# Strided attention with a squared-ReLU feed-forward: long rows for v and k, larger vector operations, both PSUM banks of the attention in one operation, five blocks by seven products

## Chip, cores, metric

One core of one Trainium2 chip. The time is device microseconds from start to end of one execution; "span" is the profiled time from the first to the last instruction. Runs are compared with runs of the kernel before of the same rounds on the same chip. Where two runs of different rounds are compared with each other, their chips can differ, so the ratios to the kernel before are the safer measure.

## The reference

```python
q, k, v = (8, 8, 576, 64) each; w_in = (512, 2048); w_out = (2048, 512)
scores = q @ k.T / sqrt(64)
# heads 0-3: the last 32 positions ("loc"); heads 4-7: every 32nd position ("str")
attn = softmax(where(mask, scores, -1e9))
x = (attn @ v), heads side by side       # (8*576 = 4608 tokens, 512)
r = maximum(x @ w_in, 0)
out = (s * r * r + b) @ w_out            # (4608, 512), float32
```

## The kernel before

The kernel is unrolled. A planner in Python (`Plan`) has assumed costs of every operation and writes out a fixed order of instructions for each engine. A software layer then adds the semaphores. Attention goes batch by batch (`b`), two heads at a time (a "pair", `m`; `loc = m < 2`). The feed-forward goes in nine blocks of 512 tokens (`T`): first product L877 (`w_in`), relu and square, second product (`w_out`). Blocks from `SEVEN` on take their second product as seven half-size products of sums and differences instead of eight; a "block by seven products" below.

The eight PSUM banks are one tile each:

```python
    TB, SB, AB, F1B, F2B = 1, 2, 1, 2, 2
    ps = {tag: [psum.tile([128, PS], FP32, name=f"ps_{tag}{i}") for i in range(n)]
          for tag, n in (("t", TB), ("s", SB), ("a", AB), ("f1", F1B), ("f2", F2B))}
    # t: transposes; s: scores; a: attention times v ("AV"); f1, f2: the two products.
    # ... from batch 4 on AV uses a and t in turn
```

Scores, exponential and mask of one group (a third of a pair), and the division after AV:

```python
                def ex(eng):                      # one group into a p buffer of its own (6 buffers)
                    nc.scalar.activation(out=pt[0:nk, 0:2 * n]..., in_=st["s", g]..., func=AF.Exp, scale=scale)
                def ms(eng):
                    nc.vector.tensor_tensor(out=pt[0:nk, 0:2 * n], in0=pt[0:nk, 0:2 * n], in1=mask, op=ALU.mult)
# ... [cut]
                def rc(eng):
                    nc.vector.reciprocal(out=st["rec", e, j]..., in_=st["pa", e, j][0:nq, 0:per, D:D + 1])
                def mu(eng):
                    nc.vector.tensor_tensor(out=st["x"][:, j0:j0 + per, 64 * e:64 * e + 64],
                        in0=st["pa", e, j][0:nq, 0:per, 0:D], in1=st["rec", e, j]..., op=ALU.mult)
```

Loads and transposed keys. GpSimd issues the loads; before those of a batch it waits, by a copy of one element, for the transposed keys of the batch before:

```python
    def fetch_qk(b):
        for mm in range(2):
            if (b - 1, "kTs", mm) in loaded:
                nc.gpsimd.tensor_copy(out=gate[0:1, 2 + mm:3 + mm], in_=loaded[b - 1, "kTs", mm][0:1, 0, 0:1])
        load_qk(b)      # from batch 4 on, k comes in 4 loads of 72 KB, in the order the transpose wants
# ... [cut]
                nc.sync.dma_start_transpose(out=st["k"][:, LPAD:LPAD + S]..., in_=loaded[b, "kl"][...])
```

The softmax here doesn't subtract the row's maximum and nothing guards it: scores larger than these inputs give would overflow.

## Time and profile before

| | before |
|---|---|
| time, median | 311.7 us (311.1 to 312.3) |
| span of the profiled run | 309.0 us |
| TensorE standstill: before 30 us, 30 to 85, after 85 | 6.3, 3.1, 0.1 us |
| useful and clock-warming matmuls (288.2 + 5.1) | 293.3 us |

Standstill is worked out from the trace: the distance from each matmul's start to the next, less what its columns take at 2.4 GHz. The prediction below explains it and shows the lines. The groups of the division (busy us, mean ns, then idle time before them):

```profile
L611 DVE TENSOR_TENSOR x_nat<-ps_a,rec 72x256 f16<-72x256 f32 (+1 forms) x52 | 23.7, 456 | 0.6
L600 DVE RECIPROCAL rec<-ps_a 72x4 f32<-72x4 f32 (+1 forms) x52 | 9.1, 176 | 6.1 <-PE ps_a L585 5.5
```

VectorE waits for AV (5.5 us).

### The profile page before, as it was taken

The page shows a single profiled execution, that of the slowest core. Times are in us where ns is not written, and L with a number is a line of the kernel's source. Part 1 is how long each engine was busy: PE and PEld are TensorE (multiplying, and loading weights), DVE is VectorE, ACT ScalarE, POOL GpSimd, SP SyncE. Part 2 cuts the span into 40 slices and gives each one's busy share as a digit, 9 for nine tenths or more (in the row PEclk, how much of TensorE's full clock was granted, in tenths as well). Part 3 has the DMA queues.
Part 4 walks back from the last instruction along what each step waited for, and adds up shares of the span by engine and source line. Part 5 has one row for each costly group of instructions (what it writes and reads, how often), then busy time and mean ns, then how long its engine had stood idle before and what let it go on. Part 6 is the DMA issues. An engine that isn't in the chain of part 4 may idle for free.

```text
span 309.0 us, 6715 instructions
## 1 busy us (share of the span) xinstructions
PE 300.5 (97%) x2526; PEld 194.4 (63%) x2526; DVE 218.2 (71%) x575; ACT 178.3 (58%) x336; POOL 99.8 (32%) x146
## 2 busy tenths in 40 slices
PE   8899999989999999999999999999999999999994
PEld 3765655555656655556687755565677666766883
DVE  7567958799976877859755874589866366737653
ACT  1876945769736964668055736694945445356300
POOL 8562559934951592059202950000000000000000
PEclk9999999999999999999999999999999999999999
DMA  7999999998999699679998999842010100200313
GB/s 127 204 212 205 216 175 159 219 135 122 99 165 176 86 147 155 110 110 183 150 174 153 128 146 159 172 92 88 2 36 34 68 2 34 104 1 0 105 67 106
DMA packets 99940, 37.28 MB, mean 121 GB/s; under 512 B 81170, under 2 KB 95890, under 8 KB 99906
## 3 DMA queue, kind: packets, MB, share of 16 engines
q0 software_dynamic: 57200, 18.08, 60.9%
q1 hardware_dynamic: 42706, 18.76, 29.9%
q8 instruction: 20, 0.33, 0.5%
q14 instruction: 14, 0.11, 0.1%
HBM read 36.84 MB, written 10.32 MB: 153 GB/s over the span
## 4 chain that ended last, share of the span: by engine, by line
PE 82%; DMA 9%; DVE 4%; issue 2%; ACT 1%; POOL 1%; SPq 0%; DVEq 0%; POOLq 0%; ACTq 0%
PE ps_f L877 35%; PE ps_f L926 20%; PE ps_f L845 12%; DMA ql<-in_q_dram 6%; PE ps_s L531 4%; PE ps_a L585 2%; DMA w_out_sb<-in_v_dram 2%; PE ps_s L845 2%; PE ps_t L585 1%; PE ps_t L845 1%; PE ps_s L926 1%; PE ps_t L411 1%; DMA out_dram<-o 1%; PE ps_t L633 1%; DVE gT L908 1%
## 5 line engine op out<-in xcount | busy, mean ns | idle before, releaser
L877 PE MATMUL ps_f<-xT,w_in_sb 128*128 128x512 f16 (+1 forms) x632 | 148.0, 357 | 0.0
L899 ACT ACTIVATE u<-ps_f 128x512 f16<-128x512 f32 x137 | 81.1, 596 | 72.8 <-PE ps_f L877 69.5
L877 PEld LDWEIGHTS <-w_in_sb 128*128 128x128 f16 x640 | 68.1, 113 | 34.5
L926 PE MATMUL ps_f<-w_out_sb,gT 128*128 128x512 f16 x304 | 80.7, 379 | 0.2 <-DVE gT L908 0.2
L908 DVE TENSOR_TENSOR gT<-u 128x512 f16<-128x512 f16 x111 | 48.1, 438 | 31.7 <-ACT u L899 30.6
L926 PEld LDWEIGHTS <-gT 128*128 128x128 f16 x320 | 28.9, 98 | 23.2 <-DVE gT L908 0.5
L845 PEld LDWEIGHTS <-gT 128*128 128x128 f16 x320 | 31.0, 98 | 8.7
L845 PE MATMUL ps_f<-w_out_sb,gT 128*128 128x256 f16 x184 | 25.9, 273 | 0.0
L611 DVE TENSOR_TENSOR x_nat<-ps_a,rec 72x256 f16<-72x256 f32 (+1 forms) x52 | 23.7, 456 | 0.6
L547 ACT ACTIVATE p_loc<-ps_s 128x384 f16<-128x384 f32 x46 | 21.1, 493 | 5.1 <-PE ps_s L531 4.8
L547 ACT ACTIVATE p_str<-ps_s 72x432 f16<-72x432 f32 (+1 forms) x46 | 21.0, 485 | 3.2 <-PE ps_s L531 2.9
L585 PEld LDWEIGHTS <-p_str 72*128 72x128 f16 x256 | 15.5, 98 | 11.2 <-issue 1.4
L906 ACT ACTIVATE gT<-u 128x512 f16<-128x512 f16 x33 | 20.8, 630 | 1.0
L293 POOL DMA_DIRECT2D v_loc<-in_v_dram x28 | 20.6, 764 | 1.8 <-DVE qD_loc L315 1.8
L937 DVE SCALAR_TENSOR_TENSOR o<-ps_f,s_sb,bcs 128x512 f32<-128x512 f32 x19 | 14.1, 747 | 9.4 <-PE ps_f L926 9.2
L298 POOL DMA_DIRECT2D v_str<-in_v_dram x16 | 13.0, 815 | 10.7 <-PE ps_a L585 3.7
L555 DVE TENSOR_TENSOR p_str<-p_str,mask_str 72x432 f16<-72x432 f16 (+1 forms) x42 | 14.7, 360 | 1.3 <-ACT p_str L547 1.0
L555 DVE TENSOR_TENSOR p_loc<-p_loc,mask_loc 128x384 f16<-128x384 f16 x42 | 14.6, 360 | 1.2 <-ACT p_loc L547 0.9
L845 PEld LDWEIGHTS <-S 128*128 128x128 f16 x128 | 12.5, 98 | 3.2
L315 ACT COPY xT<-ps_t 128x576 f16<-128x576 f16 x9 | 5.7, 637 | 13.4 <-PE ps_t L633 13.4
L600 DVE RECIPROCAL rec<-ps_a 72x4 f32<-72x4 f32 (+1 forms) x52 | 9.1, 176 | 6.1 <-PE ps_a L585 5.5
L585 PEld LDWEIGHTS <-p_loc 128*128 128x128 f16 x192 | 10.1, 98 | 5.2 <-issue 0.7
(158 smaller groups left out, 406.4 us busy)
## 6 DMA issues: line engine op xcount, KB each, us to landing
out_dram<-o SPq DMA_DIRECT2D x34, 256.0 KB, 3.1
w_out_sb<-in_moe_w_out_dram POOLq DMA_DIRECT2D x4, 512.0 KB, 11.1
v_loc<-in_v_dram POOLq DMA_DIRECT2D x28, 72.0 KB, 7.8
ql<-in_q_dram POOLq DMA_DIRECT2D x6, 288.0 KB, 6.4
qs<-in_q_dram POOLq DMA_DIRECT2D x6, 288.0 KB, 6.2
ks<-in_k_dram POOLq DMA_DIRECT2D x6, 288.0 KB, 7.6
kl<-in_k_dram POOLq DMA_DIRECT2D x4, 288.0 KB, 8.9
kl<-in_k_dram POOLq DMA_DIRECT2D x16, 72.0 KB, 3.9
```

The lines of the kernel that those rows point to most:

```text
L293: nc.gpsimd.dma_start(out=vl[LPAD:128, h, :, 0:D], in_=v_band(b, h))
L547: nc.scalar.activation(out=pt[0:nk, 0:2 * n].rearrange("k t c -> k (t c)"), in_=st["s", g][0:nk, 0:2 * n * nq], func=AF.Exp, scale=scale)
L555: nc.vector.tensor_tensor(out=pt[0:nk, 0:2 * n], in0=pt[0:nk, 0:2 * n], in1=mask, op=ALU.mult)
L585: nc.tensor.matmul(out=st["a"][:, j % per, :], lhsT=st["pw", g][0:nk, i * nq:i * nq + WIDE], rhs=vt[0:nk, 2 * mm + e, j, :])
L611: nc.vector.tensor_tensor(out=st["x"][:, j0:j0 + per, 64 * e:64 * e + 64], in0=st["pa", e, j][0:nq, 0:per, 0:D], in1=st["rec", e, j][0:nq, ...
L845: nc.tensor.matmul(out=gts[name, T, t][:, 0] if halves else gts[name, T][:, t], lhsT=lhs(k, t), rhs=rhs(k), start=fresh and k == 0 and (ha ...
L877: nc.tensor.matmul(out=gts["h", T, ft][:, lo:hi], lhsT=w_in_sb[min(ft // 4, 2)][:, ct].rearrange("p (c x l) -> p c l x", x=128, l=4)[:, ma ...
L899: nc.scalar.activation(out=gts["u", T, ft], in_=gts["h", T, ft], func=AF.Relu)
L906: nc.scalar.activation(out=gts[T][:, ft, :], in_=u, func=AF.Square)
L908: nc.vector.tensor_tensor(out=gts[T][:, ft, :], in0=u, in1=u, op=ALU.mult)
L926: nc.tensor.matmul(out=gts[id_], lhsT=gts[T][:, ft, ts * 128:(ts + 1) * 128], rhs=w_out_sb[:, ft, cols], start=(ft == 0), stop=(ft == NFT ...
L937: nc.vector.scalar_tensor_tensor(out=o[:, 0:n], in0=gts[id_], scalar=s_sb[:, 0:1], in1=bcs[:, cols], op0=ALU.mult, op1=ALU.add)
```

## The change

The intent is to take fixed costs off VectorE and GpSimd and one eighth off another block's second product. Cut to its core:

```diff
-    NX = 4                       # x of four batches in a ring
+    NX = 3
-    p_bufs: 6 tiles of one group
+    p_bufs: 2 tiles of a whole pair
-    v_str = [... for i in range(NV)]      # two
+    v_str = const.tile([SQ, 4, ST, D + 1], FP16)     # one; v of the strided heads is loaded in long rows and cast
-          for tag, n in (("t", TB), ("s", SB), ("a", AB), ("f1", F1B), ("f2", F2B))}
+          for tag, n in (("s", SB), ("f1", F1B), ("f2", F2B))}
+    ps_at = psum.tile([128, 2, PS], FP32, name="ps_at")
+    ps["a"], ps["t"] = [ps_at[:, 0]], [ps_at[:, 1]]
+    AV_WIDE = KB_DMA             # from batch 4 on
+        def both_banks(e, group):
+            got = ps_at[0:nq, :, 0:per * (D + 1)].rearrange("q u (j d) -> q u j d", d=D + 1)
+            ... one reciprocal and one multiplication for both banks
-    SEVEN = 5
+    SEVEN = 4
+            def ms(eng):         # one mask over the whole pair, behind its three exponentials
+                nc.vector.tensor_tensor(out=pt[0:nk], in0=pt[0:nk], in1=mask, op=ALU.mult)
+            def sq(eng):         # one square over two blocks of 512
+                g = gts[T][:, pair[0]:pair[0] + 2, :]
+                nc.vector.tensor_tensor(out=g, in0=u, in1=u, op=ALU.mult)     # or on ScalarE
# keys of the local heads from batch 4 on: one load of 288 KB, a copy that pairs the heads,
# the DMA transpose into kTl, and a spread into the order that the scores want
-                nc.sync.dma_start_transpose(out=st["k"][:, LPAD:LPAD + S]..., in_=loaded[b, "kl"]...)
+                nc.sync.dma_start_transpose(out=loaded[b, "kTl"][:, mm], in_=paired[b, "k"][:, mm]...)
+        def k_spread(eng):
+            copy_on(eng, out=st["k"][:, LPAD:LPAD + S]..., in_=loaded[b, "kTl"][:, mm]...)
# loads of batch 4 and later no longer held back
-            if (b - 1, "kTs", mm) in loaded:
+            if (b - 1, "kTs", mm) in loaded and b < FREE_FROM + 2:          # FREE_FROM = 2
# assumed latency of every early DMA 12 us instead of 5.5
-  (5500.0 if eng == "D" and end < 110000.0 else self.LAT[eng])
+  self.LAT[eng]
```

## The prediction

> **What bounds the kernel now.** I read four views in this order: the slices of the span on the page, the windows of 10 us, the chain of waits in order of time, and the timeline around the few places where TensorE stands still. First, four rows of the slices:
>
> ```profile
> PE   8899999989999999999999999999999999999994
> DVE  7567958799976877859755874589866366737653
> ACT  1876945769736964668055736694945445356300
> DMA  7999999998999699679998999842010100200313
> ```
>
> TensorE is busy throughout, but its records overlap, so "busy" alone doesn't show that it runs at its peak. The windows (us; busy time and instructions of PE, PE weight loads, DVE, ACT, POOL; clock, DMA share, GB/s) show where it is not busy:
>
> ```profile
> 0.00:10.00 10.00, 8.48 (x73) 3.96 (x73) 6.98 (x29) 3.11 (x5) 7.00 (x15) 1.00 0.89 144
> ...
> 60.00:70.00 10.00, 9.05 (x88) 5.51 (x88) 9.39 (x24) 7.55 (x16) 4.35 (x6) 1.00 1.21 158
> 70.00:80.00 10.00, 9.69 (x85) 5.88 (x84) 9.89 (x24) 8.76 (x19) 6.23 (x11) 1.00 0.77 112
> ...
> 190.00:200.00 10.00, 10.00 (x51) 5.00 (x50) 4.52 (x11) 5.94 (x10) 0.00 (x0) 1.00 1.08 170
> ```
>
> The reader is to see three stages: a head of some 30 us, a stretch around 60 to 80 us (57 to 85 by the single pauses below) in which VectorE is 94 to 99% busy and TensorE is not full, and from 85 us on a full TensorE. Whether "full" is "at its peak" is read from the spacing of the matmuls, which the chain in order of time gives (start, us, what):
>
> ```profile
> 232.42 0.86 PE ps_f L877 x4
> 233.28 0.76 PE ps_f L845 x7
> 234.04 0.86 PE ps_f L877 x4
> 234.91 0.77 PE ps_f L845 x7
> ```
>
> One 512-column matmul costs 0.86/4 = 0.216 us and one of 256 columns 0.765/7 = 0.109 us. I took the distance from each matmul's start to the next in the timeline, and subtracted what its columns need at this rate (columns/2.4 ns + 2 ns, at least 32 ns). The rest is standstill: 9.4 us in the whole span, of which 6.3 before 30 us, 0.8 from 30 to 57 us (eight pauses of 0.1 us), 2.3 from 57 to 85 us, and under 0.1 us in the 220 us after that. The clock-warming matmuls of the head (L1162) are another 5.1 us. Useful matmul work is 288.2 us of 309.0. From 85 us to the end the time is therefore the sum of the matmuls, and no wait of any other engine can shorten it.
>
> The 2.3 us are in five places (59.7, 62.2, 64.8, 75.9 and 84.8 us), and all wait for VectorE:
>
> ```profile
> PE ps_t L411 <- DVE qD_str L315: 0.7, 1, 0.7
> PE ps_a L585 <- DVE x_nat L611: 0.5, 2, 0.3
> PE ps_f L926 <- DVE gT L908: 0.2, 1, 0.2
> ```
>
> The timeline tells why VectorE is late there. While GpSimd copies, squares that otherwise take 0.42 us take 0.98 and 1.04:
>
> ```profile
> 62.54 0.84 POOL L315 COPY qp<-ql 96x768 f16<-96x768 f16 x1
> 62.68 1.95 DVE L908 TENSOR_TENSOR gT<-u 128x512 f16<-128x512 f16 x2
> 62.81 0.35 PE L585 MATMUL ps_a<-v_loc,p_loc 128*128 128x65 f16 x6 [0.20 <-DVE x_nat L611]
> ```
>
> **What the Trainium skill says.** "Perfetto Trace Analysis", section "Identifying the Most-Contended Engine", calls matmul busy time a bad measure of distance to the roofline; the trace agrees, since L877's mean record is 357 ns while its spacing is 216. "TensorE: Matmul & The Clock Gate", section "Wait — 56ns, not 53.3ns?", gives a warm spacing of N/2.4 GHz + about 2.5 ns, which is 215.7 ns at 512 columns and 109.2 at 256; the trace agrees (216 and 109). "VectorE: DVE Perf Modes", sections "The TRN2 errata" and "The perf-mode tier table", says that a fixed cost is paid per instruction, so larger tiles pay it once, and that tensor_tensor on 16-bit SBUF data runs at twice the base rate. The trace agrees: 384 elements take 350 ns (L555, median) and 1024 take 685 (L717), that is 0.523 ns an element, two per cycle of 0.96 GHz, and about 149 ns fixed. "DMA: Bandwidth & Descriptors", section "Why small descriptors are slow (HBM only)", names a fixed overhead per packet; this kernel has 81170 of its 99940 packets below 512 B, but the trace shows no late wait of TensorE on them.
>
> **The change, part by part.**
>
> *Five blocks by seven products (SEVEN 5 to 4).* Block 4's second product now takes 64 matmuls of 512 columns, 64 x 0.216 = 13.82 us. It becomes 7 x 16 = 112 matmuls of 256 columns, 112 x 0.109 = 12.21 us. This is on the path, because TensorE is saturated there (F2 of block 4 runs from 181 to 213 us): **-1.6 us**. VectorE gains 8 sums of 0.685 (5.5 us), and the evictions grow from 4 of 0.75 to 7 of 0.75 and one of 0.69 (+2.9 us). The mixing of the weights (4 x 1.2 us) moves from about 213 to about 181 us. VectorE was idle 5.5 us of the ten at 190 to 200 and saves elsewhere, so I count nothing against it.
>
> *A ring of three instead of four batches for x.* Block 4 no longer straddles the ring's end, but blocks 3 and 6 do; 64 matmuls split in two become 128. Two halves cost 2 x 109 = 218 for 216 ns, so **+0.1 us**. The last batch's x must also wait for block 5's first product. That ended at 208 us and the x transposes began at 205, while block 7, which reads it, starts at 240: hidden.
>
> *Larger operations on VectorE.* Squares in pairs: 2 x 421 = 842 becomes one of 685 ns, 157 saved. Masks over a whole pair of heads: three of 350 become one of 1152 elements, 685 + 128 x 0.523 = 752 ns by estimate, 298 saved. In the tight stretch there are 16 squares and 18 masks: 8 x 0.157 + 6 x 0.298 = 3.0 us of VectorE time, against 2.3 us of standstill. The stalls are at five separate places and the AV products of a pair must now wait for all three exponentials and the one wide mask, so I take two thirds as won back: **-1.5 us**. The divisions over two banks begin with batch 4 (24 fewer reciprocals and 24 fewer multiplications, some 24 x (0.15 + 0.15) = 7 us of VectorE time); they and all later squares and masks lie beside a saturated TensorE and give nothing.
>
> *Long rows for k and v from batch 4.* 32 loads of 72 KB become 8 of 288 KB. GpSimd saves 32 x 0.78 - 8 x 0.69 = 19 us of issuing. In exchange come 8 pair copies (0.35 on VectorE or 0.93 on GpSimd), 8 spreads (0.64 on ScalarE or 0.75) and 16 casts (0.40), some 14 us over three engines, all after 85 us: **0**.
>
> *Loads not held back.* GpSimd's waits on the transposed keys (35.0 us, six times) vanish. Nothing on TensorE waited for the late loads, so **0**. The longer assumed latency of early DMAs only reorders; no standstill came from a DMA there.
>
> *New waits:* one strided v buffer instead of two, both banks at once for a division, transposes among unheld loads: **+0.3 us**, a judgement. Head and tail keep their shape: 0.
>
> Sum: 312.1 - 1.6 + 0.1 - 1.5 + 0.3 = **309.4 us**, -0.9%.
>
> **The rivals.**
>
> *VectorE or a buffer becomes a bound in 170 to 215 us.* Seven-product sums and weight mixing now fall on the last batch's attention. For it: VectorE is 90% busy at 170 to 180 and 200 to 210 before. Against it: masks, squares and divisions save there more than the 8 us that come. It would make standstill of 1 to 4 us: 310.5 to 313.5.
>
> *The relief of the tight stretch doesn't come.* The bigger operations lengthen each chain from exponential to AV product by some 0.4 us, and GpSimd's copies, which stretch the neighbours on VectorE, stay. Then only the seventh product counts: 310.6.
>
> *The unheld loads slow the transposes.* x transposes already take 9.3 us to land, and the DMA engines are most loaded between 90 and 190 us. For it: the hold was put there for something. Against it: block 5 reads x at 181 us that was sent by 167, and block 6 at 213 what was sent by 200, over 10 us of slack. It would make 310 to 314.
>
> *All stalls after 30 us and some of the head go.* 312.1 - 1.6 - 3.1 = 307.4; half a microsecond of fewer start-up memsets could add to it. Below this I see no mechanism.
>
> **Range and chances.** The first step is nearly arithmetic. The spread comes from the 2.3 us of stall (0 to all), new stalls (0 to 2) and the head (half a microsecond each way): 307.2 to 311.4. Faster by over 2% means below 305.8, which needs more than every stall after the head: 4%. Slower by over 2% means above 318.3, some 8 us of new stall in a stage that had none: 2%. Within 2%: 94%.
>
> **What would show it right or wrong.** Right: 448 + 112 = 560 matmuls at L845's place and 256 at L926's; wide squares near 0.69 us and wide masks near 0.75; standstill of TensorE from 57 to 85 us below 1 us; spacing still 216 and 109 ns afterwards, without gaps; GpSimd's gate waits gone with no effect on the end. Wrong: any TensorE wait after 90 us on v_str, the x ring, an AV bank or a DMA, or a head of other length than some 30 us, which I didn't foresee moving.

## The result

The changed kernel takes **341.2 us** (336.4 to 344.3, 4 runs) against 311.7; the ratio of the fast runs is 1.085, 95% interval 1.074 to 1.097. (Ratios here are the mean time of one kernel's fast runs over that of the other's of the same rounds, so not quite the ratio of the medians quoted.) The prediction of 309.4 was wrong, in direction too. Two of the changed kernel's four runs are labelled slow, because they are over 1.5% above the fastest; they are not in the ratio. The profiled run is the fastest of the four (336.4 us); its span is 334.6 us, 25.6 more. Why the others take up to 8 us longer isn't explained here. First the rows of the slices, as before:

```profile
PE   7779899798789799999978996999999999999995
DVE  5276675576686676687748885856636545836662
ACT  2565884276772788688757892464362463455300
DMA  8999999997934994999999642201400100110113
```

TensorE is no longer full for as long as attention lasts, and no other engine took its place as the bound: VectorE and ScalarE are idler than before in the same stretch. In the windows of 10 us:

```profile
70.00:80.00 10.00, 8.37 (x85) 4.96 (x83) 7.50 (x15) 7.22 (x15) 5.08 (x6) 1.00 0.75 108
80.00:90.00 10.00, 7.77 (x72) 4.36 (x71) 6.22 (x13) 7.17 (x12) 5.49 (x8) 1.00 1.10 123
200.00:210.00 10.00, 7.32 (x43) 3.50 (x42) 5.24 (x8) 2.32 (x5) 0.00 (x0) 0.83 0.23 58
```

When nothing is busy and the time still grows, engines wait for each other in turn. TensorE's standstill rose from 9.4 to 36.2 us, +26.8, which is the whole loss of this run: +4.4 before 30 us, +5.7 from 30 to 85, +16.6 after. Of the 25.5 us after 30 us, 16.1 end at a matmul that writes `ps_at`. Before 30 us such matmuls end 6.3 us of standstill, against 1.5 for the two banks in the kernel before; in two_tiles below it is 1.6 again, so the head's 4.4 us belong to the tile too. TensorE's waits (us in total, times, longest) name what released it:

```profile
PE ps_at L621 <- DVE x_nat L605: 2.7, 1, 2.7
PE ps_at L621 <- ACT qD_loc L313: 2.1, 2, 1.1
PE ps_at L413 <- DVE x_nat L652: 2.1, 5, 0.6
PE ps_at L677 <- DVE x_nat L652: 1.9, 2, 1.5
```

Line 1 is a wait for an x buffer, not for the tile; more on it below. Line 2 is odd. L621 is AV, which in batches 2 and 3 writes bank a alone. L313's `qD_loc` copies transposed queries out of bank t. Line 3 is the same the other way: L413 transposes into bank t and waits for L652, a division that reads bank a. The timeline around 111 us shows it step by step (the division there is the narrow one, of six values a row, so its AV is from before batch 4 and in bank a):

```profile
110.79 0.25 PE L413 MATMUL ps_at<-ident,qp 96*128 96x96 f16 x2
...
111.08 0.19 DVE L641 RECIPROCAL rec<-ps_at 96x6 f32<-96x6 f32 x1 [0.68 <-PE ps_at L413]
111.32 0.33 PE L413 MATMUL ps_at<-ident,qp 96*128 96x96 f16 x4 [0.28 <-DVE rec L641]
...
111.69 0.55 DVE L652 TENSOR_TENSOR x_nat<-ps_at,rec 96x384 f16<-96x384 f32 x1 [0.42 <-PE ps_at L413]
...
112.28 1.28 ACT L313 COPY qD_loc<-ps_at 64x576 f16<-64x576 f16 x2 [0.88 <-DVE x_nat L652]
...
113.61 0.35 PE L621 MATMUL ps_at<-v_loc,p_loc 128*128 128x65 f16 x6 [1.09 <-ACT qD_loc L313]
```

Six transposes into bank t stop after the second, until a reciprocal of bank a has been read; that reciprocal had itself waited for the second transpose. The multiplication waits for the other four transposes, the copy of bank t for the multiplication of bank a, and the next AV for that copy. Neither the reciprocal and the transposes nor the copy and the AV share a byte or a bank. They share a tile.

The rest of the loss has other causes: 2.8 us at 203 us (line 1, so it is among the 16.1), where a division waits for an x buffer (4.1 us for `DMA xT<-x_nat`), then seven matmuls at half clock (1.5 us), and some 4 us at 170 to 178 us: keys (1.2 and 0.6), an exponential (1.4) and x (0.9).

What was forecast of the parts holds in this profile. There are 256 matmuls of the direct second product and 560 by seven products. The larger operations have the durations worked out:

```profile
L961 DVE TENSOR_TENSOR gT<-u 128x1024 f16<-128x1024 f16 x48 | 33.0, 687 | 25.8 <-ACT u L951 25.0
L605 DVE TENSOR_TENSOR x_nat<-ps_at,rec 72x512 f16<-72x512 f32 (+1 forms) x24 | 18.5, 772 | 4.5 <-DMA xT<-x_nat 4.1
L564 DVE TENSOR_TENSOR p_loc<-p_loc,mask_loc 128x1152 f16<-128x1152 f16 x14 | 10.3, 745 | 0.1
```

### The profile page after: what moved, and what is told of

It reads as the page before. It is cut to its first block, busy times and chain, and to the rows that moved or that the text cites.

```text
span 334.6 us, 6663 instructions
## 1 busy us (share of the span) xinstructions
PE 306.8 (92%) x2641; PEld 203.8 (61%) x2641; DVE 214.4 (64%) x439; ACT 189.9 (57%) x331; POOL 78.0 (23%) x109
## 4 chain that ended last, share of the span: by engine, by line
PE 78%; DVE 7%; DMA 6%; ACT 6%; issue 2%; SPq 1%; DVEq 0%
PE ps_f L924 32%; PE ps_f L892 15%; PE ps_f L982 11%; DMA kTl<-kp 4%; PE ps_s L538 4%; PE ps_at L621 3%; PE ps_at L413 2%; PE ps_f L1214 2%; PE ps_at L892 2%; ACT qD_loc L313 2%; DMA xT<-x_dram 2%; PE ps_s L892 2%; DVE x_nat L652 1%; ACT u L951 1%; PE ps_at L677 1%
## 5 line engine op out<-in xcount | busy, mean ns | idle before, releaser
L924 PE MATMUL ps_f<-xT,w_in_sb 128*128 128x512 f16 (+4 forms) x696 | 147.7, 340 | 1.0 <-DMA xT<-x_dram 0.7
L982 PE MATMUL ps_f<-w_out_sb,gT 128*128 128x512 f16 x240 | 65.5, 387 | 0.5 <-ACT gT L959 0.5
L961 DVE TENSOR_TENSOR gT<-u 128x1024 f16<-128x1024 f16 x48 | 33.0, 687 | 25.8 <-ACT u L951 25.0
L959 ACT ACTIVATE gT<-u 128x1024 f16<-128x1024 f16 x24 | 25.4, 1058 | 0.6
L605 DVE TENSOR_TENSOR x_nat<-ps_at,rec 72x512 f16<-72x512 f32 (+1 forms) x24 | 18.5, 772 | 4.5 <-DMA xT<-x_nat 4.1
L621 PEld LDWEIGHTS <-p_str 72*128 72x128 f16 x256 | 13.5, 98 | 9.1 <-issue 3.6
L538 PE MATMUL ps_s<-qD_loc,kT_loc 128*128 128x192 f16 x92 | 14.5, 251 | 2.4 <-ACT p_loc L556 1.3
L764 DVE TENSOR_TENSOR gT<-gT 128x1024 f16<-128x1024 f16 x22 | 14.6, 685 | 1.3 <-ACT gT L959 1.3
L652 DVE TENSOR_TENSOR x_nat<-ps_at,rec 72x256 f16<-72x256 f32 (+1 forms) x29 | 13.2, 457 | 2.9 <-ACT qD_loc L313 1.3
L621 PE MATMUL ps_at<-v_str,p_str 72*128 72x65 f16 x208 | 12.6, 194 | 2.2 <-DVE kT_loc L313 1.1
L621 PEld LDWEIGHTS <-p_loc 128*128 128x128 f16 x192 | 8.5, 98 | 9.5 <-issue 6.6
L538 PEld LDWEIGHTS <-kT_loc 128*128 128x128 f16 x96 | 9.1, 102 | 8.4 <-issue 2.0
```

The costliest lines, as they stand in the source:

```text
L538: nc.tensor.matmul(out=st["s", g][0:nk, c:c + 2 * nq], lhsT=(st["k"][:, i * nq:i * nq + nk] if loc else st["k"][:, i, 0:SQ]), rhs=st["q"][ ...
L605: nc.vector.tensor_tensor(out=x, in0=got[:, :, :, 0:D], in1=st["rec", e][0:nq, :, 0:per].to_broadcast([nq, 2, per, D]), op=ALU.mult)
L621: nc.tensor.matmul(out=st["a"][:, j % per, :], lhsT=st["pw", g][0:nk, i * nq:i * nq + WIDE], rhs=vt[0:nk, 2 * mm + e, j, :])
L924: nc.tensor.matmul(out=gts["h", T, ft][:, lo:hi], lhsT=w_in_sb[min(ft // 4, 2)][:, ct].rearrange("p (c x l) -> p c l x", x=128, l=4)[:, ma ...
L959: nc.scalar.activation(out=g, in_=u, func=AF.Square)
L961: nc.vector.tensor_tensor(out=g, in0=u, in1=u, op=ALU.mult)
```

## The experiments

**Theory 1:** the one tile `ps_at` makes accesses to its two banks wait for each other. **Theory 2:** the ring of three, the single v buffer or the new order of issue costs the time. **Theory 3:** the loads that aren't held back slow the DMA transposes.

| run | what it is | median, us | ratio to before (95%) |
|---|---|---|---|
| after | the changed kernel | 341.2 | 1.085 (1.074 to 1.097) |
| two_tiles | changed, two tiles, no wide division, order mended | 314.1 | 1.007 (1.005 to 1.009) |
| one_tile_narrow | same, one tile | 343.1 | 1.101 (1.095 to 1.106) |
| after_held | changed, order mended only | 334.8 | 1.076 (1.070 to 1.083) |
| before_one_tile | before, one tile for a and t | 342.7 | 1.099 (1.094 to 1.104) |
| before_s_one | before, one tile for the score banks | 326.3 | 1.047 (1.045 to 1.048) |
| two_gated | two_tiles, loads held | 314.3 | 1.008 (1.005 to 1.011) |
| two_short_k | two_tiles, old path of the keys | 311.5 | 1.001 (0.998 to 1.003) |
| two_spread_cost | two_tiles, measured costs in the plan | 314.4 | 1.009 (1.007 to 1.012) |
| two_single_sq | two_tiles, single squares | 323.6 | 1.039 (1.036 to 1.042) |
| before_seven4 | before, SEVEN = 4 | 310.3 | 0.996 (0.994 to 0.997) |
| before_masks | and one mask per pair | **309.3** | 0.993 (0.990 to 0.996) |
| masks_pairs | and squares in pairs | 310.1 | 0.995 (0.993 to 0.997) |
| masks_free | before_masks, loads not held | 325.0 | 1.043 (1.039 to 1.048) |
| best_seven3 | before_masks, SEVEN = 3 | 324.7 | 1.041 (1.039 to 1.043) |
| seven3_free | that, loads not held | 325.1 | 1.042 (1.038 to 1.046) |

All gave correct results. The kernel before had medians of 311.6 to 311.8 in these rounds. The medians are over all runs, the ratios over the fast ones; slow were two of four runs of the changed kernel, two of seven of two_gated, two of 14 of two_short_k and one of six of seven3_free.

### The tile

`two_tiles` gives the two banks back their own tiles. Without the wide division the order that comes out can't be built: a division needs an x buffer whose reader, an x transpose, is issued later (a deadlock). So an AV chain is ordered behind that transpose as well. `one_tile_narrow` has both edits but keeps the tile; the pair differs in the tile alone.

```diff
-    AV_WIDE = KB_DMA
+    AV_WIDE = B                                    # never
+            x_held = [("xT", b - 1, m)] if b and e == j == 0 else []     # added to AV's needs
-    ps_at = psum.tile([128, 2, PS], FP32, name="ps_at")                  # two_tiles only
-    ps["a"], ps["t"] = [ps_at[:, 0]], [ps_at[:, 1]]
+          for tag, n in (("t", TB), ("s", SB), ("a", AB), ("f1", F1B), ("f2", F2B))}
```

> The changed kernel with the PSUM banks 'a' and 't' as two tiles again instead of the halves of one tile; the division over both banks, which needs the one tile, is off; an AV chain's first matmul is ordered behind the x transpose that frees its x buffer (without that the order of issue deadlocks). Theory 1 (one tile makes accesses to its two banks wait for each other): 308 to 311 us, standstill of TensorE after 30 us under 3 us, waits of ps_a on readers of ps_t gone. Theory 2 (the ring of three for x, the single v buffer or the new order of issue is to blame): stays above 325. Theory 3 (unheld loads slow the transposes): stays above 325 with TensorE waiting for DMA.

> As two_tiles, but with the one tile of two banks kept: only the tile differs. Theory 1: 328 to 345 us, with ps_at written by PE waiting for readers of the other bank. Theory 2 or 3: the same time as two_tiles within 2%. If instead the wide division itself (which needs both banks free at once) were the cost: 308 to 312 here too.

Measured: 314.1 and 343.1 us. The two traces hold the same instructions in the same order on every engine, so the tile alone is worth 29.0 us. Standstill after 30 us is 5.4 us in the one and 31.5 in the other, of which 27.0 before a matmul into `ps_at`. Two_tiles missed its range of 308 to 311, by 3 us, and the standstill forecast (under 3 us after 30 us); this is followed up below. Theories 2 and 3 as the main cause are out.

The plainest form of the test leaves everything else of the kernel before as it was:

```diff
-          for tag, n in (("t", TB), ("s", SB), ("a", AB), ("f1", F1B), ("f2", F2B))}
+          for tag, n in (("s", SB), ("f1", F1B), ("f2", F2B))}
+    ps_at = psum.tile([128, 2, PS], FP32, name="ps_at")
+    ps["a"], ps["t"] = [ps_at[:, 0]], [ps_at[:, 1]]
```

> The kernel before with nothing changed but ps_a and ps_t made the two halves of one PSUM tile; the order of issue is identical. Theory 1: 325 to 340 us, that is +13 to +28, most of it between 30 and 210 us while attention runs. Theories 2 and 3: 312 us, unchanged.

Measured: 342.7 us, +30.8, a little over the range. I compared the two traces instruction by instruction: all 2526 matmuls and the instructions of VectorE, ScalarE and GpSimd come in the same order on the same data. Two lines of declaration cost 10%. Its waits of TensorE:

```profile
PE ps_at L587 <- DVE x_nat L613: 5.8, 9, 1.2
PE ps_at L413 <- DVE x_nat L613: 4.2, 6, 1.0
PE ps_at L587 <- ACT qD_loc L315: 3.2, 4, 1.3
```

In the kernel before no line of this view that concerns these two banks is over 0.7 us; the largest are in the prediction. Is it the tile, or the 16-bit view through which bank t is written? The two score banks are always 32-bit and used in turn:

```diff
+    ps_s2 = psum.tile([128, 2, PS], FP32, name="ps_s2")
+    ps["s"] = [ps_s2[:, 0], ps_s2[:, 1]]
```

> The kernel before with the two score banks ps_s0 and ps_s1 made the halves of one tile, ps_a and ps_t left apart; order of issue identical. Score banks are written and read as 32-bit values and used in turn, so this asks whether the false wait belongs to any tile of two banks. If so: 318 to 345 us, scores waiting for the exponential that reads the other half. If it came from the 16-bit views of bank t: 312.

Measured: 326.3 us, +14.6, again in the same order of instructions.

```profile
PE ps_s L533 <- ACT p_loc L549: 3.4, 8, 1.2
PE ps_s L533 <- ACT p_str L549: 2.6, 8, 0.4
```

Scores for one bank wait for the exponential that reads the other: the double buffer is gone. So the rule, as far as these runs reach, is about a PSUM tile that spans two banks, in this software layer. It is not a property of the banks: the Trainium skill, "PSUM — Partial Sum Buffer", section "Summary: rules for kernel authors", says to read PSUM under a running matmul from a different bank and to guard by bank, and the kernel before does just that at full TensorE rate.

### The order mended, the wide division kept

```diff
+            x_held = [("xT", b - 1, m)] if b and e == j == 0 else []
```

> The changed kernel with only the order mended: an AV chain starts behind the x transpose that frees its x buffer. The profile after has one standstill of 2.8 us at 203 us there, followed by seven matmuls at half clock (1.5 us). Theory 1: 2 to 5 us less than the changed kernel, so 333 to 339. If the x ring of three were the main cost: below 325.

Measured: 334.8 us (334.1 to 338.7), inside the 333 to 339 expected. The changed kernel's median is 6.4 above, but two of its four runs are slow: its fast runs average 338.3 us against 335.6 here, 2.7 less, and the intervals of the two ratios overlap. The trace is clearer: the pause at 203 us and the slow matmuls behind it are gone, and standstill after 85 us fell from 16.7 to 14.6. The ring of three was therefore not hidden, as the prediction had it; it was a minor part. A by-product: after_held and one_tile_narrow differ in the wide division only, and with it the kernel is 8.2 us faster. Standstill before matmuls into `ps_at` after 30 us is 13.5 us with it and 27.0 without, in 23 pauses over 0.1 us against 51: probably because dividing both banks at once means fewer exchanges between them. The wide division relieved some of the damage that its tile did.

### What is left: two_tiles is 314.1, not 309.4

Four runs undo one part of two_tiles each, or mend one number. The profiled run of two_tiles took 312.0 us, at the low end of its twenty (312.0 to 316.0), so its trace shows less of the loss than the median.

```diff
-    FREE_FROM = 2
+    FREE_FROM = B                                   # two_gated: loads held as before
```

> two_tiles with the loads of q and k from batch 4 on held back again until the transposes of the batch before have landed (FREE_FROM 8 for 2). two_tiles took 314.1 us, some 4 more than predicted without the tile's cost, and its profile has a 1.75 us standstill at 152 us on keys whose transpose took 9.8 us to land while GpSimd issued a burst of loads. If the unheld loads slow the transposes: 310 to 312.5, key transposes landing in under 6 us, that standstill gone. If not: 314 again.

Measured: 314.3, no change, although the keys' transposes now landed in 5.1 us instead of up to 9.8. The standstill at 152 us went and others came (1.0 us at 85 us, 0.8 and 0.7 on first-product matmuls at 190 to 194 us). In this kernel, holding or not holding is worth nothing that the runs can tell.

```diff
-                if (b, "kTl") not in loaded: ...      # two_short_k: no pair copy, no spread
+                nc.sync.dma_start_transpose(out=st["k"][:, LPAD:LPAD + S]..., in_=loaded[b, "kl"]...)
```

> two_tiles with the local keys from batch 4 on loaded and transposed as in the kernel before: four loads of 72 KB in the order the transpose wants, no pair copy, no spread. The prediction gave the new path 0 us. If the path's two more steps make the keys late: 310 to 312. If not: 314.

Measured: 311.5 us, 2.6 less by the medians, 2.0 by the ratios, whose intervals don't meet. Standstill after 85 us fell from 3.2 to 1.4 us. The longer path of the keys is not free. These are two_tiles' waits for it:

```profile
PE ps_s L536 <- DVE kT_loc L313: 1.6, 1, 1.6
...
PE ps_s L536 <- ACT kT_loc L313: 0.3, 1, 0.3
```

```diff
-            {"V": 757.0, "A": 660.0}, k_spread      # two_spread_cost
+            {"V": 650.0, "A": 1180.0}, k_spread
```

> two_tiles with only the assumed costs of spreading the transposed keys set to what the traces show: 0.65 us on VectorE (assumed 0.757) and 1.18 us on ScalarE (assumed 0.66), so that the order of issue counts on the right times. If the wrong cost puts score matmuls ahead of their keys: 312 to 313, waits of scores for kT_loc under 0.5 us (1.9 before). If not: 314.

Measured: 314.4, no change. One wait of 0.5 us for `kT_loc` was left, but a first-product matmul then waited 1.6 us for an x transpose, and the head was longer. A wrong cost in the plan (ScalarE needs 1.18 us for this spread, 0.66 assumed) was not what mattered.

```diff
-                    {"V": 700, "A": 1055}, sq over a pair     # two_single_sq
+                    {"V": 430, "A": 600}, sq of one block, six buffers
```

> two_tiles with the squares one block of 512 at a time again (six single buffers instead of three of two blocks). The wide squares were forecast to save VectorE time and cost nothing; but in two_tiles TensorE waited 0.5 us for a wide square on ScalarE at 86 us and 1.0 for a bank that ScalarE's relu frees. If wide squares delay the second product's inputs: 311 to 313. If not: 314, or more if VectorE lacks the 157 ns a pair.

Measured: 323.6 us, a surprise and no answer. The new order put a copy of batch 2's queries on GpSimd behind memsets and loads that lasted from 51 to 59 us, and TensorE waited for it:

```profile
PE ps_t L411 <- POOL qp L313: 8.0, 1, 8.0
```

So squares were tested from the other side, starting from the kernel before.

### The parts, added to the kernel before

```diff
-    SEVEN = 5
+    SEVEN = 4                                        # before_seven4
```

> The kernel before with only SEVEN = 4: five blocks by seven products. By the prediction's first step 13.82 - 12.21 = 1.6 us less: 310.2 us, ratio 0.995, with no new standstill after 85 us. Rival (VectorE becomes a bound at 170 to 215 us by sums and weight mixing): 312 or more, with TensorE waiting for VectorE there.

Measured: 310.3 us, -1.3 (ratio 0.996). The first step of the prediction holds. The rival of a VectorE bound at 170 to 215 us doesn't show: one new pause of 0.4 us came there, at 193 us, and it waits for ScalarE's `u`.

```diff
+ ex, ms and p_bufs of the change                     # before_masks
```

> before_seven4 plus one mask operation per pair of heads instead of three (and the p buffers of a whole pair that this needs). By the prediction's third step the masks are 1.8 of the 3.0 us that VectorE saves at 57 to 85 us: 309.0 us, standstill there 1.2 us or less (2.3 before). Rival (the longer chain from exponential to AV product eats it): 310 or more, with TensorE waiting for p_loc or p_str.

Measured: 309.3 us; the interval (0.990 to 0.996) overlaps that of before_seven4, and the standstill in the profiled run is the same 2.9 us from 30 to 85 us. The gain of the masks is likely but not shown. This is the lowest median of all, below both kernels.

```diff
+ rl and sq of the change, with up bufs=2             # masks_pairs
```

> before_masks (309.3 us) plus the squares two at a time, in two buffers of two blocks in place of four of one. By the prediction the wide squares save VectorE 1.3 us between 57 and 85 us: 308.5 us. Rival: TensorE waits for the second of each pair and for relus behind 1.06 us squares on ScalarE: 310 to 312, with waits of the second product for gT or of the first for ScalarE's u.

Measured: 310.1 us, not the 308.5 forecast, not separable from before_masks. Standstill from 30 to 85 us did fall, from 2.9 to 1.7 us, but 1.1 us came after 85 us, part of it on the second square of a pair (`PE ps_f` waiting for `DVE gT`). Relief and delay cancel, as far as these runs can tell.

```diff
-            if (b - 1, "kTs", mm) in loaded:
+            if (b - 1, "kTs", mm) in loaded and b < 4:      # masks_free; also no wait on them in the plan
```

> before_masks with the loads of batch 4 and later not held back for transposed keys. By the prediction nothing on TensorE waited for these loads: 309.3 us, within half a microsecond. If unheld loads slow the transposes: 310.5 or more, TensorE waiting for kT or xT.

Measured: 325.0 us, +15.7: a miss by far, and the larger part of it is on neither of the paths that I had named. Its GpSimd issues the small loads early and waits between them:

```profile
137.67 0.83 POOL L298 DMA_DIRECT2D v_str<-in_v_dram  x1
141.41 1.68 POOL L298 DMA_DIRECT2D v_str<-in_v_dram  x2 [2.91 <-DMA kl<-in_k_dram]
145.80 0.80 POOL L298 DMA_DIRECT2D v_str<-in_v_dram  x1 [2.71 <-DMA x_dram<-x_nat]
146.65 1.38 POOL L315 COPY qD_str<-qT 64x576 f16<-64x576 f16 x2
```

The releasers named for these waits, a load of k and a store of x, can't free a v buffer; that the loads wait for buffers still in use is my reading, not shown. The spread of queries in the last line lies behind them on the same engine, and TensorE waits for it (first line below):

```profile
PE ps_s L531 <- POOL qD_str L315: 7.1, 1, 7.1
...
PE ps_t L588 <- DVE x_nat L614: 4.1, 1, 4.1
```

The second line is the rival that I had named after all: at 108.6 us AV waits for a division, and the division for an x transpose:

```profile
112.50 0.56 DVE L614 TENSOR_TENSOR x_nat<-ps_t,rec 96x384 f16<-96x384 f32 x1 [4.73 <-DMA xT<-x_nat]
```

In before_masks no division waits for an x transpose. Whether the early loads slowed this one was not tested. After the two pauses (7.3 and 4.3 us from start to start) some dozen matmuls of 512 columns come at half clock (2.5 us); with 0.7 us for a key transpose at 174 us, that is nearly all of the 15.7.

The Trainium skill, "TensorE: Matmul & The Clock Gate", in the table at its head, calls GpSimd's queue strict first-in first-out; the trace agrees, with 7.1 us here and 8.0 in two_single_sq. In before_masks the hold kept such loads out of this spread's way. With long rows there are few loads to get in the way, which may be why two_tiles and two_gated are alike and the two parts of the change belong together; no run tests that. Two_short_k has short rows for k and no hold, and no such pause, so if rows matter, it is those of v.

```diff
-    SEVEN = 4
+    SEVEN = 3                                        # best_seven3; seven3_free has the edit of masks_free too
```

> before_masks with SEVEN = 3: six blocks by seven products instead of five. before_seven4 gave 1.3 us for one block, so another 1.3 to 1.6 us: 307.8 us, ratio 0.988 to the kernel before. Rival: block 3's second product runs while three batches of attention are still to come, and VectorE's 8 us more make TensorE wait: 309 to 311.

> best_seven3 (324.7 us) with the loads not held back. There TensorE stood still for 13.0 us at 174.6 us because a spread of queries on GpSimd lay behind twelve load issues that the hold had delayed to 171 us. If the hold is the cause: that standstill is gone and the time is 307.5 to 309.5. If GpSimd's queue is blocked by the small loads anyway: above 315.

Measured: 324.7 and 325.1. (The expectation counts twelve load issues; the trace of best_seven3 has eighteen between 171.5 and 186.2 us.) The matmul work fell by another 1.6 us as forecast (290.0 us against 291.6), and standstills of 13.0 us (at 174.6 us, behind GpSimd's `qD_str`) in the one and of 5.2, 3.8 and 3.7 us in the other took it back. My attribution to the hold fell with the second run. Queue order on GpSimd stands as what the first run waited for; what else is late in the second (3.5 us for `kT`; 5.0 for `x_nat`, whose division again waits for an x transpose, as in masks_free) I didn't follow further.

## Why the prediction was wrong

- **"What bounds the kernel now"** was right (one slip: the 357 ns set against a spacing of 216 is a mean over two widths; the 512-column records last 379 ns), and before_one_tile makes the same point from the other side: with the same instructions in the same order, the time is the sum of the matmuls plus whatever makes TensorE wait.
- **Seven products, -1.6 us:** right; 1.3 us by before_seven4, and 1.6 us less matmul work in the traces of before_seven4 and before_masks.
- **"New waits: ... both banks at once for a division ... +0.3 us, a judgement":** this is the step that failed. I read the one tile as a matter of space for one wide operation and asked when both banks would be free. I didn't ask what the tile is to the layer that sets the semaphores. It costs 29.0 us (one_tile_narrow against two_tiles), 30.8 us in the kernel before. None of my rivals contained it; of the signs of being wrong, a wait on "an AV bank", on the x ring, and a longer head all came. The wait that I did price, both banks at once, isn't what costs: with one tile the wide division is 8.2 us faster than the narrow one.
- **A ring of three, "hidden":** wrong by a few us. The wait was not for the ring itself at block 7, but one step upstream: an x transpose held by the ring holds one of two x buffers, and a division needs it (2.8 us standstill; 2.7 us between the fast runs of the changed kernel and after_held).
- **Larger operations, -1.5 us:** durations right (687 ns for 685; 745 and 782 for 752). In two_tiles TensorE is busy for 27.94 us of the 28 from 57 to 85 us, 26.74 before, so the tight stretch was relieved. But wide squares brought delays elsewhere, and the net of the squares is zero within the error (masks_pairs).
- **Long rows, 0:** wrong by 2.0 to 2.6 us for the keys. I put the copies "beside" the work, by busy time, and didn't add up the length of their path. The spread on ScalarE takes 1.18 us, not 0.64.
- **Loads not held back, 0:** right for the change (two_gated), but by luck: without the long rows, on top of before_masks, it costs 15.7 us. "Nothing on TensorE waited for the late loads" says what removing a delay gains. It doesn't say what the earlier loads will push back.

What stays open: of the 4.8 us between two_tiles and before_masks, the keys' path accounts for 2.6 (by the ratios 2.0 of 4.4). The other 2.2 (single v buffer, ring of three, added order, squares, and whatever else of the change two_tiles keeps) I didn't divide. It is also open whether a wide operation over two banks could be had without the shared tile; no such version was built.

## What to carry to other kernels

Under a layer that sets semaphores by tile, as this one appears to, buffers that should be used independently should be separate tiles: joining two PSUM banks in one tile for the sake of one wide operation tied together every access to both, and cost 29 us where the operations that it widened had next to nothing to save, TensorE being full there. A loss with every engine idler than before can come from false dependences, as here: look in the timeline for two instructions that wait for each other's neighbour, and test by changing only the declaration. In a queue that is strictly in order, loads that are moved earlier and then wait hold up every compute step behind them (7.1 us in masks_free), and gains off the bound are worth nothing until their path is measured.

## What the Trainium skill lacked or had wrong

- "PSUM — Partial Sum Buffer" gives the hardware's rule, to guard by bank. No page that I read says that a software layer may guard a PSUM tile of two banks as one. The runs show +30.8 us (before_one_tile) and +14.6 us (before_s_one) at the same order of instructions.
- "TensorE: Matmul & The Clock Gate", section "Back-to-back issue gap", gives a sustained spacing of about 131 ns at 512 columns and 81 ns at 128 for pairs of weight load and matmul. In two_tiles, each with its own weight load, 512 columns take 216 ns and 128 columns 56 ns (median of 64, start to start), which the page gives for isolated matmuls, and the 65-column AV matmuls 33 ns.
- The same page, section "What's actually happening", has the clock fall after an idle window of about 3.4 us. In the changed kernel a pause of 3.1 us between two matmul starts (202.8 to 205.9 us; 2.7 us without a running matmul) was followed by twelve small matmuls and two of 512 columns, and then by seven of 512 columns 427 ns apart, twice the normal. So less than a full such window of idleness was enough.
